# A narrow transpose placed before ScalarE's cast of its PSUM bank, and a multiplication placed three steps later

## The chip, the cores and the metric

The kernel runs on one core of a Trainium2 chip. The metric is the device time of one execution in microseconds (us); a change is given against the median of three runs. TensorE is called PE here (its weight loads PEld), VectorE DVE, ScalarE ACT, GpSimd POOL, and SyncE, which issues most DMAs, SP.

## The reference

Three layers follow one another, all in 32-bit floats:

- Attention over 2 batches x 8 heads, 768 tokens, head size 64. Each query and key gets a 6-bit bucket (the signs of its projections); a query sees only keys of its bucket: `scores = where(q_bucket == k_bucket, q k^T / 8, -1e9)`, then a softmax over the keys and a product with v.
- `x = relu(x @ w_in)**2 @ w_out` with 1536 tokens, 512 features and 2048 hidden units.
- The same shapes again with `h * sigmoid(h)` in place of the squared relu.

## The kernel before

The 16 heads are worked in 8 pairs. A pair has 4 units (head h, query half z of 384), a unit has 3 score tiles (128 queries x 768 keys) and 6 key blocks of 128. The attention is a software pipeline of steps d (`for d in range(-5, G // 2 + 3)`, L1258): 12 steps per pair, step 12(p+1) being the first step of the pair after p. In each step the program emits, engine by engine in this order:

- DVE: the row maximum of the score tile made in the step before (L996), the low part of the previous key block (`t_lo`, L1036), two small operations that make scale and bias of the exponential (L1000, L1001), then `t_lo` of the step's first block.
- PE: for two key blocks three 128x128 transposes each of the exponentials P (`transp`, L1025) into PSUM tiles `t` (three bank-sized buffers); four matmuls of v with the transposed blocks two behind (`av`, L1049, L1050); and four matmuls of the next score tile (`score_mm`, L989; its third and fourth use the rows of the bucket bits in `qq` and `kk`).
- ACT: the high part of each transposed block (`t_hi`, L1030, a cast out of the bank), and the exponential (L1009), which also gives the row sums.

A product is kept to float precision by splitting operands into a high and a low part.

Once per pair there is a long step, at 12(p-1)+5 for the pair p to come: PE also computes the projections of its queries and keys (`bits_mm`, 12 matmuls, L789), DVE compares them with zero (`bits_cmp`, L795, after a first `t_lo`, with the second `t_lo` between the two compares), and SP sends the bits to their rows of `qq` and `kk` (`place_bits`, L919, the `kk` part second). The first score that reads them is issued two steps later. In the long steps 17, 29, 41, 53, 65 and 77 there are also one or two DVE operations that prepare weights of the next layer (`w_exp` L958, `w_sign` L962, `w_low` L966).

The softmax is normalised on the product side. `norm_rows` (step 2 of the next pair) takes the reciprocals of a pair's 12 columns of sums on DVE. For pairs 0 to 5 `row_turn` (step 5 of the next pair, so in the six long steps just named, called turns below) transposes them on PE into columns 384 to 511 of the bank of the step's second block, whose first 384 columns `t_hi` reads, and ACT copies them out. `row_put` sends them to DRAM, and three steps later `row_get` reads them back spread over 64 partitions each into `rw` (two buffers). `x_mul` (POOL, step 10) multiplies the pair's summed output `ta` (two buffers) by `rw` into `yf`; `x_put` (POOL, step 10) splits a part of that into `xk`, once for pairs 0 to 3 and twice for 4 and 5.

Each engine runs its own instructions in the order in which they are emitted. Behind `x_mul` and `x_put` on POOL come `split_pair` for the keys (L774, step 11), whose result SP sends on (L779, L780), `load_head` (L764, step 1 of the pair after, a DMA issued by POOL) and `x_sum` of the next pair (L1103, step 3 of that pair), which frees `tb` (one buffer) for DMAs that SP issues (L1062).

The lists `todo` (end of a step) and `mid` (inside it) hold what else a step emits; within a step of `todo` the entries of the loop over `p` in L1141 come first. After the attention PE starts the two layers; their order is planned once and is the same in both kernels.

Of the kernel before, what the change touches and what calls it, by code (L numbers as in the profile page):

```python
# [24 lines left out]
NPAIR = B * H // 2  # L25
NU = NPAIR * 4
QW = 384
# [672 lines left out]
def lsh_attention_moe_moe(ctx, tc, kd, qk, qf, fq, v, pc, wi1, wo1, wi2, wo2, out):  # L700
    nc = tc.nc
# [23 lines left out]
    ident = ac.tile([128, 128], F32, name="ident")  # L725
# [30 lines left out]
    def scale_q(p):  # L756
        q = pair[p]["r"][0]
        nc.scalar.mul(out=q, in_=q, mul=SCALE)
# [23 lines left out]
    def bits_mm(p):  # L782
        t = pair[p]
        hp, lp = t["hp"], t["lp"]
        ops = [(w[:, 48 * i : 48 * i + 48], x) for i in range(2) for (w, x) in ((pjh, hp[i]), (pjl, hp[i]), (pjh, lp[:, i]))]
        s = ps_s.tile([128, 2, 512], F32, tag="s", name=f"bs{p}")[:, 0], ps_t.tile([128, 512], F32, tag="t", name=f"bt{p}")
        for z in range(2):
            for j, (w, x) in enumerate(ops):
                mm(s[z][0:48, 0:QW], w, x[:, z * QW : (z + 1) * QW], start=j == 0, stop=j == 5)  # L789
        return s  # L790
# [185 lines left out]
    P, stats, otile, sums = {}, {}, {}, {}  # L976

    def warm_up(n):
        for _ in range(n):
            mm(warm, zb[:, 0:128], zb[:, 0:512], start=True, stop=True)  # L980
# [13 lines left out]
    def row_max(u, j, s):  # L994
        m = mt[:, (u * 3 + j) % 4]
        nc.vector.tensor_reduce(out=m[:, 0:1], in_=s[:, :, 0:QW], op=ALU.max, axis=AX.XY, negate=True)  # L996
        return m

    def row_live(m):
        nc.vector.tensor_scalar(out=m[:, 1:2], in0=m[:, 0:1], scalar1=LIM, scalar2=1.0, op0=ALU.is_lt, op1=ALU.mult)  # L1000
        nc.vector.tensor_scalar(out=m[:, 2:3], in0=m[:, 0:1], scalar1=LIM, scalar2=m[:, 0:1], op0=ALU.is_lt, op1=ALU.mult)  # L1001

    def score_exp(u, j, s, m):
        p = u // 4
        if u % 4 == 0 and j == 0:
            sums[p] = a2.tile([128, 12], F32, tag="sums", name=f"sums{p}")
        e = P[u, j] = ac.tile([128, S], F32, tag="P", bufs=6, name=f"P{u}_{j}")
        c = (u % 4) * 3 + j
        nc.scalar.activation(  # L1009
            out=e.rearrange("p (a b) -> p a b", a=2),  # L1010
            in_=s[:, :, 0:QW],
            func=AF.Exp,
            scale=m[:, 1:2],
            bias=m[:, 2:3],
            accum_out=sums[p][:, c : c + 1],
        )

    PT = {}

    def transp(g, t=None):  # L1020
        u, kt = divmod(g, KT)
        if t is None:
            t = ps_t.tile([128, 512], F32, tag="t", name=f"t{g}")
        for j in range(3):
            nc.tensor.transpose(t[:, j * 128 : (j + 1) * 128], P[u, j][:, kt * 128 : (kt + 1) * 128], ident)  # L1025
        PT[g] = (t,)

    def t_hi(g):
        th = a1.tile([128, QW], F32R, tag="th", bufs=6, name=f"th{g}")
        nc.scalar.copy(out=th, in_=PT[g][0][:, 0:QW])  # L1030
        PT[g] += (th,)

    def t_lo(g):
        t, th = PT[g]
        tl = a1.tile([128, QW], F32R, tag="tl", bufs=6, name=f"tl{g}")
        nc.vector.tensor_tensor(out=tl, in0=t[:, 0:QW], in1=th.bitcast(F32), op=ALU.subtract)  # L1036
        PT[g] = th, tl
# [3 lines left out]
    def av(g):  # L1041
        u, kt = divmod(g, KT)
        p, h, z = u // 4, (u // 2) % 2, u % 2
        if kt == 0:
            otile[u] = ps_o.tile([128, 512], F32, tag="o", name=f"o{u}") if u < NU - 1 else ps_s.tile([128, 2, 512], F32, tag="s", name=f"o{u}")[:, 0]
        o = otile[u]
        vv = pair[p]["vv"][:, h * KT + kt].rearrange("p a d -> p (a d)")
        th, tl = PT.pop(g)
        mm(o[:, 0:QW], vv, th, start=kt == 0, stop=False)  # L1049
        mm(o[:, 0:QW], vv, tl, start=False, stop=kt == KT - 1)  # L1050
        if kt == KT - 1:
            if p not in xs:
                xs[p] = [a1.tile([128, S], F32, tag=n, bufs=b, name=f"{n}{p}") for n, b in (("ta", 2), ("tb", 1))]
            if u == NU - 1:
                ta, zs = xs[p][0], slice(z * QW, (z + 1) * QW)
                nc.scalar.copy(out=ta[64:128, zs], in_=o[0:64, 0:QW])
                nc.vector.tensor_tensor(out=ta[64:128, zs], in0=o[64:128, 0:QW], in1=ta[64:128, zs], op=ALU.add)
                return
            ob = a2.tile([128, QW], F32, tag="ob", name=f"ob{u}")
            nc.scalar.copy(out=ob, in_=o[:, 0:QW])  # L1060
            for i in range(2):
                nc.sync.dma_start(out=xs[p][i][64 * h : 64 * h + 64, z * QW : (z + 1) * QW], in_=ob[64 * i : 64 * i + 64])  # L1062
# [10 lines left out]
            w = rows[p] = a1.tile([128, 6, 2, 64], F32, tag="rw", bufs=2, name=f"rw{p}")  # L1073
            nc.gpsimd.tensor_copy(out=w, in_=ri.rearrange("p (h c) -> p c h", h=2).unsqueeze(3).broadcast_to([128, 6, 2, 64]))

    def row_turn(p, t):
        nc.tensor.transpose(t[0:12, QW:512], sums[p], ident)
        r = turned[p] = a1.tile([12, 128], F32, tag="rt", name=f"rt{p}")
        nc.scalar.copy(out=r, in_=t[0:12, QW:512])

# [54 lines left out]
    long, scale, turn = {}, {}, {}  # L1135
    last = defaultdict(list)

    def at(g, fn, *a):
        todo[g].append((fn, a))
# [21 lines left out]
    for p in range(NPAIR):  # L1161
        d0 = 12 * (p + 1)
        at(d0 + (-3 if p < NPAIR - 1 else -4), norm_sums, p)
        at(d0 + (2 if p < NPAIR - 1 else -3), norm_rows, p)
        at(d0 + (3 if p < NPAIR - 1 else 0), x_sum, p)
        if p == NPAIR - 2:
            extra[d0 + 9].append((rb_mm, x_norm, p))
            at(d0 + 10, x_mul, p)
            at(d0 + 10, x_put, p)
        elif p < NPAIR - 2:  # L1170
            k = d0 + 5
            turn[k] = p
            at(k, row_put, p)
            at(k + 3, row_get, p)
            at(k + 5, x_mul, p)
            at(k + 5, x_put, p)

    for k, d in enumerate(X_STEPS):
        at(d, x_form, k)
# [14 lines left out]
    with tc.manual_schedule():  # L1194
# [15 lines left out]
        c, k = slice(64, 64 + NBR), first["c"]  # L1210
# [47 lines left out]
        for d in range(-5, G // 2 + 3):  # L1258
            ready, new = new, None
            g = 2 * d  # L1260
            if ready:
                m = row_max(*ready)
            if 0 <= g - 1 < G and g - 1 not in early_lo:
                t_lo(g - 1)
            if ready:
                row_live(m)
            for fn, a in mid.pop(d, []):
                fn(*a)
            if 0 <= g < G and d in (92, 94):
                t = ps_s.tile([128, 2, 512], F32, tag="s", name=f"t{g}")  # L1270
                for i in range(2):
                    transp(g + i, t[:, i])
                t_hi(g)
                t_hi(g + 1)
                t_lo(g)
            elif 0 <= g < G:
                transp(g)
                t_hi(g)
                t_lo(g)
                transp(g + 1)  # L1280
                t_hi(g + 1)
                if d in turn:
                    row_turn(turn[d], PT[g + 1][0])
            more = extra.pop(d, [])
            if ready and more and d not in long:
                score_exp(*ready, m)
            if d in long:
                score_exp(*ready, m)
                if d in scale:
                    scale_q(scale.pop(d))  # L1290
            for n in (g - V_LAG, g + 1 - V_LAG):
                if 0 <= n < G:
                    av(n)
            if d in long:
                t = bits_mm(long[d])
            held = [(dve, pe(p), p) for pe, dve, p in more]
            if d in long:
                bits_cmp(t, long[d], 0)
                t_lo(g + 1)
                bits_cmp(t, long[d], 1)  # L1300
            for dve, t, p in held:
                dve(t, p)
            if ready and not more and d not in long:
                score_exp(*ready, m)
            u, j = divmod(d + 5, 3)
            if u < NU:
                new = u, j, score_mm(u, j)
            for fn, a in todo.pop(d, []) + last.pop(d, []):
                fn(*a)
            warm_up(WARM.get(d, 0))  # L1310
        p = NPAIR - 1
        for z in (1, 0):
            t = ps_t.tile([128, 512], F32, tag="t", name=f"rb{p}_{z}")
# [12 lines left out]
        t = dict(yf=yf, xk=xk, wpa=wpa, raw=raws, wt=wt, pair=both, src=((wi1, wo1), (wi2, wo2)), out=out)  # L1326
# [58 lines left out]
```

## Time and profile before

| what | value |
|---|---|
| median of 3 runs (lowest to highest) | 729.46 us (729.27 to 729.68) |
| the profiled execution | 728.33 us, span from first to last instruction 726.6 us |
| busy share of the span: PE, PEld, DVE, ACT, POOL | 98%, 84%, 84%, 74%, 36% |
| chain that ended last | PE 80%, DVE 15%, ACT 3%, issue 1% |
| granted TensorE clock | 1.000 |
| end of the attention | about 235.3 us |

The busy shares are means over both stages. The chain of waits goes back from the last instruction to what released each one. A row of a timeline gives the start, the duration, the engine, the line, the operation with its tiles, and in brackets how long the engine had been idle before it and what ended that; rows of instructions of one line that follow each other are merged (x6). Matmuls are pipelined: a row's duration is longer than the time to the next start.

### The profile page before, as it was taken

The numbers are of one execution on the slowest core, as the hardware profiler recorded it, in microseconds if no ns is written. First come the engines' busy times: TensorE is split into PE (matmuls) and PEld (weight loads), VectorE is DVE, ScalarE is ACT, GpSimd is POOL, SyncE is SP. The second block draws the span as 40 slices with busy tenths as digits, with TensorE's granted clock in tenths as the row PEclk, the third lists the DMA queues.
The fourth block names the chain that finished last, engine by engine and source line by source line (L and its number), as shares of the span: only waits on it lengthen the run. The fifth ranks groups of instructions, "written<-read, shape, count | busy, mean of one in ns | idle before, by whom it ended". The sixth has DMA issues, their size and how long they took to land.

```text
span 726.6 us, 10910 instructions
## 1 busy us (share of the span) xinstructions
PE 714.7 (98%) x3643; PEld 612.2 (84%) x3643; DVE 610.8 (84%) x1106; ACT 539.7 (74%) x1012; POOL 258.7 (36%) x242
## 2 busy tenths in 40 slices
PE   8999999999999999999999999999999999999998
PEld 4999898898899888888888888888788888888886
DVE  7999999999998979786797879989778778888840
ACT  6998898898798898486459568878766945854861
POOL 7634755656547512041231223234203110212300
PEclk9999999999999999999999999999999999999999
DMA  5887698697662536124534653368231332345432
GB/s 172 202 199 169 158 204 187 153 222 175 147 157 55 122 107 169 59 73 102 130 88 116 133 134 96 87 143 172 70 124 58 88 89 80 107 102 116 102 110 93
DMA packets 38640, 92.16 MB, mean 127 GB/s; under 512 B 5564, under 2 KB 10524, under 8 KB 38584
## 3 DMA queue, kind: packets, MB, share of 16 engines
q1 hardware_dynamic: 26120, 67.18, 31.7%
q0 software_dynamic: 12032, 23.79, 18.3%
q8 instruction: 29, 0.48, 0.3%
q10 hardware_dynamic: 432, 0.49, 0.2%
q14 instruction: 27, 0.22, 0.1%
HBM read 51.96 MB, written 3.18 MB: 76 GB/s over the span
## 4 chain that ended last, share of the span: by engine, by line
PE 80%; DVE 15%; ACT 3%; issue 1%; DMA 0%; POOL 0%; ACTq 0%; DVEq 0%; POOLq 0%
PE bank L558 36%; PE bank L443 24%; DVE mt L996 7%; PE bank L420 7%; DVE tl L1036 6%; PE s L989 3%; PE t L1025 3%; PE o L1049 2%; PE o L1050 2%; ACT P L1009 2%; PE bs L789 1%; PE bt L789 1%; DVE mt L1001 1%; ACT th L1030 1%; DVE mt L1000 1%
## 5 line engine op out<-in xcount | busy, mean ns | idle before, releaser
L558 PE MATMUL bank<-woh,cell 128*128 128x512 f32 (+1 forms) x392 | 120.0, 385 | 0.0
L558 PE MATMUL bank<-cell,woh 128*128 128x512 f32 x384 | 118.3, 389 | 0.0
L1036 DVE TENSOR_TENSOR tl<-t,th 128x384 fp32r<-128x384 f32 x192 | 104.7, 548 | 0.8 <-ACT th L1030 0.8
L1009 ACT ACTIVATE P<-s,mt 128x768 f32<-128x768 f32 x96 | 95.3, 993 | 11.2 <-DVE mt L1001 8.1
L996 DVE TENSOR_REDUCE mt<-s 128x1 f32<-128x768 f32 x96 | 91.5, 953 | 3.5 <-PE s L989 3.1
L1030 ACT CAST th<-t 128x384 fp32r<-128x384 f32 x192 | 81.9, 483 | 12.5 <-PE t L1025 12.1
L558 PEld LDWEIGHTS bank<-woh,cell 128*128 128x128 f32 x392 | 73.1, 188 | 14.7
L558 PEld LDWEIGHTS bank<-cell,woh 128*128 128x128 f32 x384 | 72.1, 188 | 15.2
L989 PE MATMUL s<-kk,qq 76*128 76x384 f32 (+1 forms) x384 | 83.8, 339 | 0.5 <-ACT P L1009 0.4
L1025 PE MATMUL t<-ident,P 128*128 128x128 f32 x576 | 78.9, 272 | 0.0
L278 DVE TENSOR_TENSOR cell<-bank,cell 128x512 f32<-128x512 f32 x91 | 62.1, 692 | 18.3 <-PE bank L443 13.9
L443 PE MATMUL bank<-xw,wpb 128*128 128x512 f32 x312 | 75.9, 389 | 0.0
L558 PE MATMUL bank<-wol,cell 128*128 128x512 f32 (+1 forms) x196 | 75.4, 385 | 0.0
L558 PE MATMUL bank<-cell,wol 128*128 128x512 f32 x192 | 74.7, 389 | 0.0
L1049 PE MATMUL o<-th,vv 128*128 128x384 f32 x192 | 72.5, 377 | 0.0
L1025 PEld LDWEIGHTS t<-ident,P 128*128 128x128 f32 x576 | 67.8, 140 | 4.5 <-DVE tl L1036 0.2
L989 PEld LDWEIGHTS s<-kk,qq 76*128 76x128 f32 (+1 forms) x384 | 68.3, 188 | 2.6 <-ACT P L1009 1.6
L443 PEld LDWEIGHTS bank<-xw,wpb 128*128 128x128 f32 x312 | 58.5, 188 | 12.4 <-DVE bank L278 0.3
L1050 PE MATMUL o<-tl,vv 128*128 128x384 f32 x192 | 64.3, 335 | 0.0
L588 ACT COPY yf<-bank 128x512 f32<-128x512 f32 x48 | 27.9, 586 | 35.4 <-PE bank L558 34.7
L450 ACT COPY cell<-bank 128x512 f32<-128x512 f32 x39 | 22.9, 587 | 40.7 <-PE bank L443 38.7
L268 ACT CAST cell<-cell 128x512 fp32r<-128x512 f32 x81 | 48.8, 617 | 1.9 <-DMA cell<-cell 0.8
(201 smaller groups left out, 1484.8 us busy)
## 6 DMA issues: line engine op xcount, KB each, us to landing
raw<-in_dram SPq DMA_DIRECT2D x64, 512.0 KB
cell<-cell POOLq DMA_DIRECT2D x23, 256.0 KB, 3.4
qq<-hq SPq DMA_DIRECT2D x28, 192.0 KB
kk<-in_dram POOLq DMA_DIRECT2D x14, 384.0 KB, 5.3
yf<-cell POOLq DMA_DIRECT2D x21, 256.0 KB, 3.3
vr<-in_dram SPq DMA_DIRECT2D x8, 384.0 KB
ta<-ob SPq DMA_DIRECT2D x31, 96.0 KB
tb<-ob SPq DMA_DIRECT2D x31, 96.0 KB
```

What stands on the lines that cost most here:

```text
L278: add("DVE", 0.70, lambda: vec.tensor_tensor(out=val(out), in0=bank[b], in1=val(other), op=ALU.add), [("bank", b), *reads], writes)
L420: mm(bank[b], wpa[n][:, p, 4 * h + j], x[:, q], start=j == 0 and z == 0, stop=j == 3 and z == 2)
L443: mm(bank[b], w[:, p], x[:, q], start=not started and z == 0, stop=z == 2, skip_group_check=started)
L558: mm(bank[b][:, 0:wd], x, y, start=start and i == 0 and z == 0, stop=i == (FB if half is None else 2 * half + 2) - 1 and z == 2, skip_grou ...
L989: mm(s[:, n, 0:QW], t["qq"][h][0:kk, ab, c0 : c0 + 128], t["kk"][h][0:kk, ab, n * QW : (n + 1) * QW], start=ab == 0, stop=ab == 1)
L996: nc.vector.tensor_reduce(out=m[:, 0:1], in_=s[:, :, 0:QW], op=ALU.max, axis=AX.XY, negate=True)
L1009: nc.scalar.activation(out=e.rearrange("p (a b) -> p a b", a=2), in_=s[:, :, 0:QW], func=AF.Exp, scale=m[:, 1:2], bias=m[:, 2:3], accum_ou ...
L1025: nc.tensor.transpose(t[:, j * 128 : (j + 1) * 128], P[u, j][:, kt * 128 : (kt + 1) * 128], ident)
L1030: nc.scalar.copy(out=th, in_=PT[g][0][:, 0:QW])
L1036: nc.vector.tensor_tensor(out=tl, in0=t[:, 0:QW], in1=th.bitcast(F32), op=ALU.subtract)
L1049: mm(o[:, 0:QW], vv, th, start=kt == 0, stop=False)
L1050: mm(o[:, 0:QW], vv, tl, start=False, stop=kt == KT - 1)
```

## The change

Two things change. The narrow transpose of the reciprocals is issued by PE right behind the transposes of the second block, ahead of the program's `t_hi` of that block; ACT's copy of its result stays behind `t_hi`. And for pairs 0 to 4 `x_mul` goes from step 10 to step 13 (counted from the start of the next pair, so step 1 of the one after), and `x_put` from step 10 to step 14. Pair 5 keeps both at step 10.

```diff
-    def row_turn(p, t):
-        nc.tensor.transpose(t[0:12, QW:512], sums[p], ident)
+    def row_copy(p, t):
         r = turned[p] = a1.tile([12, 128], F32, tag="rt", name=f"rt{p}")
         nc.scalar.copy(out=r, in_=t[0:12, QW:512])
...
-            at(k + 5, x_mul, p)
-            at(k + 5, x_put, p)
+            x = k + (8 if p < NPAIR - 3 else 5)
+            at(x, x_mul, p)
+            at(x + 1 if p < NPAIR - 3 else x, x_put, p)
...
                 transp(g + 1)
+                if d in turn:
+                    nc.tensor.transpose(PT[g + 1][0][0:12, QW:512], sums[turn[d]], ident)
                 t_hi(g + 1)
                 if d in turn:
-                    row_turn(turn[d], PT[g + 1][0])
+                    row_copy(turn[d], PT[g + 1][0])
```

## Rows read from the trace of the kernel before

**Rows 1.** Busy time by engine in the stretch behind the attention (PE, PEld, DVE, ACT, POOL).

```profile
235.30:726.60 491.30, 487.56 (x2161) 403.38 (x2159) 389.32 (x578) 336.43 (x568) 118.70 (x107) 1.00 0.41 107
```

**Rows 2.** Who waited for whom: total us, times, longest.

```profile
PE t L1077 <- ACT th L1030: 6.2, 6, 1.0
```

**Rows 3.** Timeline of PE, step 16, the turn in step 17, and step 19.

```profile
50.59 0.82 PE L1025 MATMUL t<-ident,P 128*128 128x128 f32 x6
...
51.95 0.86 PE L989 MATMUL s<-kk,qq 128*128 128x384 f32 x4
52.64 0.82 PE L1025 MATMUL t<-ident,P 128*128 128x128 f32 x6
54.50 0.27 PE L1077 MATMUL t<-ident,sums 128*12 128x128 f32 x1 [1.04 <-ACT th L1030]
...
55.31 0.33 PE L789 MATMUL bs<-hq,pjh 128*48 128x384 f32 x1
...
57.40 0.88 PE L989 MATMUL s<-kk,qq 128*128 128x384 f32 x4
...
61.54 0.69 PE L989 MATMUL s<-kk,qq 128*128 128x384 f32 x3
```

**Rows 4.** Timeline of DVE, the row maximum in step 19.

```profile
60.38 0.96 DVE L996 TENSOR_REDUCE mt<-s 128x1 f32<-128x768 f32 x1 [0.34 <-PE s L989]
```

**Rows 5.** Timeline of ACT in the turn of step 17.

```profile
53.50 0.86 ACT L1030 CAST th<-t 128x384 fp32r<-128x384 f32 x2
54.81 0.26 ACT L1079 COPY rt<-t 12x128 f32<-12x128 f32 x1 [0.45 <-PE t L1077]
```

**Rows 6.** Timeline of DVE in the turns of steps 17, 29 and 77.

```profile
55.43 0.55 DVE L1036 TENSOR_TENSOR tl<-t,th 128x384 fp32r<-128x384 f32 x1
56.56 0.67 DVE L795 TENSOR_SCALAR bt<-bs,tmt 48x384 fp32r<-48x384 f32 x1 [0.58 <-PE bs L789]
...
82.46 0.68 DVE L966 SCALAR_TENSOR_TENSOR wi<-raw,wi 128x512 uint32<-128x512 uint32 x1
...
83.40 0.55 DVE L1036 TENSOR_TENSOR tl<-t,th 128x384 fp32r<-128x384 f32 x1
84.66 0.67 DVE L795 TENSOR_SCALAR bt<-bs,tmt 48x384 fp32r<-48x384 f32 x1 [0.71 <-PE bs L789]
...
194.90 1.70 DVE L966 SCALAR_TENSOR_TENSOR both<-raw,both 128x512 uint32<-128x512 uint32 x1
...
196.86 0.55 DVE L1036 TENSOR_TENSOR tl<-t,th 128x384 fp32r<-128x384 f32 x1
197.32 0.66 DVE L795 TENSOR_SCALAR bt<-bs,tmt 48x384 fp32r<-48x384 f32 x1
```

**Rows 7.** Timeline of SP's DMA issues in the same three long steps.

```profile
59.15 1.06 SPq L919 DMA_DIRECT2D kk<-bt  x1
...
87.27 0.76 SPq L919 DMA_DIRECT2D kk<-bt  x1
...
199.91 0.77 SPq L919 DMA_DIRECT2D kk<-bt  x1
```

**Rows 8.** Line L989 after steps 29 and 77: PE sequencer's waits, ns, start us.

```profile
L989 PEldq EVENT_SEMAPHORE  x1: 752/752/752, 88.8 to 88.8; - x1
...
L989 PEldq EVENT_SEMAPHORE  x1: 857/857/857, 201.4 to 201.4; - x1
```

**Rows 9.** Timeline of PE, the first scores of a pair after steps 29 and 77.

```profile
89.64 0.68 PE L989 MATMUL s<-kk,qq 128*128 128x384 f32 x3
...
202.07 0.86 PE L989 MATMUL s<-kk,qq 128*128 128x384 f32 x4
```

**Rows 10.** Timeline of POOL before the turn of step 77.

```profile
185.96 1.84 POOL L1115 TENSOR_TENSOR yf<-rw,ta 128x768 f32<-128x768 f32 x1 [6.39 <-DMA rw<-rows]
...
191.72 1.85 POOL L774 TENSOR_TENSOR lp<-rk,hk 128x768 fp32r<-128x768 f32 x1
...
194.20 1.84 POOL L1103 TENSOR_TENSOR ta<-ta,tb 128x768 f32<-128x768 f32 x1
```

## The prediction

> **What bounds the kernel now.** I read the page first (busy shares and the chain that ended last, in the table above), then busy time by stretch, then who waited for whom, and then timelines of one turn and the steps around it, engine by engine. Behind the attention PE is busy 487.56 of 491.30 us [rows 1]: that stage is TensorE back to back, so whatever the attention saves should reach the end unchanged. In the list of waits the reader is to look for PE as the one that waits: the narrow transpose waited for ACT's cast six times, 6.2 us in all, the longest 1.0 [rows 2]. All six turns are therefore alike.
>
> Who sets the pace of a plain step? PE's starts repeat after 2.05 us (50.59 to 52.64) [rows 3]. Of that the score takes 0.69 (51.95 to 52.64), and four value matmuls 0.70, at the 0.174 that one 384-column matmul of the projections takes (twelve from 55.31 to 57.40) [rows 3]. That leaves 0.66 for the six transposes, 0.11 each. DVE needs nearly as long, but two steps after the turn it stands idle for 0.34 us until PE has a score ready [rows 4]. PE leads, DVE follows closely. An engine that follows by so little may take over when PE gets faster, so both are followed below.
>
> **The transpose.** In the turn of step 17 PE begins its six transposes at 52.64; they occupy it for 0.66, so it could go on at 53.30. The narrow transpose starts at 54.50 [rows 3]. PE loses 1.20 us; the 1.04 in the row is smaller because the profile lets the last transpose end later. Nothing else in the step waits: ACT's second cast, which held the bank, runs from about 53.93 to 54.36 [rows 5]. Moved ahead of that cast, the narrow transpose needs only the reciprocals, made three steps earlier. It follows at 53.30 and still costs its 0.11. Six turns give 6 x 1.20 = 7.2 us.
>
> The wait turns round: now the second cast waits for the narrow transpose. Behind it on ACT stand the copy (0.26), the exponential and the rest of the step. PE finishes the narrow transpose at about 53.30 + 0.27 = 53.57, and the second cast could not begin before 53.93 since the first one runs until then [rows 5]. It is covered with about 0.36 to spare; uncovered it would delay an engine that idles 0.45 right there [rows 5]. I cost it at nothing. ACT's copy then loses its 0.45 of waiting and the exponential starts earlier.
>
> **What is late next: the bits.** With PE 1.20 earlier, the projections, the compares on DVE, SP's two DMAs and the first score that reads them all want to move up by 1.20. DVE cannot quite. In step 17 its `t_lo` at 55.43 hands on after 0.46 (196.86 to 197.32, where nothing waits), so the first compare can start at 55.89 instead of 56.56: 0.67 earlier, not 1.20. In step 29, 83.40 + 0.46 = 83.86 against 84.66: 0.80 earlier [rows 6]. What follows (second compare, DMA issues, landing) moves with the compare.
>
> How much slack had the bits? PE's sequencer sat in a semaphore wait for them until 88.8 + 0.75 = 89.6 and until 201.4 + 0.86 = 202.23 [rows 8]; the issues of the `kk` bits ended at 88.03 and 200.68 [rows 7]. So they land 1.55 to 1.57 us after the issue ends. In the first turn that gives 59.15 + 1.06 + 1.56 = 61.77, 0.23 after the score's first matmul at 61.54, and PE's row shows no wait [rows 3, 7]; the third matmul is the first to read them. I take 0.2 after the first matmul as the deadline. Then the slack was about 0 in step 17, 89.84 - 89.6 = 0.24 in step 29, and 202.27 - 202.23 = 0.04 in step 77 [rows 8, 9].
>
> So PE gets a new wait two steps after each turn. Step 17: 1.20 - 0.67 - 0 = 0.53. Step 29, and step 53 with the same two weight operations: 1.20 - 0.80 - 0.24 = 0.16 each. Step 77 depends on the next part and gives 0.14. Steps 41 and 65, with one weight operation, I take at 0.1 each. Sum 1.2 us. Its bounds: nothing, if the DMA issue shortens or the landing is quicker (the issue ran from 0.76 to 1.06 [rows 7]), and 6 x 1.20 = 7.2 if the compares do not move at all. I take 1.2, which lies nearest to the rows of the turns themselves.
>
> **x_mul and x_put.** POOL is told to multiply at step 10, before the rows are back from DRAM, and stands idle: 6.39 us before the multiplication of pair 4 [rows 10]. Behind it wait the key split and the DMA of the next head, then `x_sum`. The only one of PE's waits that is large is the one for ACT's cast [rows 2]; none is for POOL. So the stall itself costs nothing and its removal gives nothing directly. In number: five `x_mul` of 1.84, and `x_put` pairs of a cast and a subtraction, move past one key split and one head load each, no SP instruction of their own; no work is added. The split and its two SP DMAs come earlier by several us, with no reader before the next pair.
>
> There is one indirect effect. In step 77 the weight operation L966 took 1.70 us; in step 29 it took 0.68. At 194.90, when it started, POOL was in `x_sum` (194.20 to 196.04), late because of the queue before it [rows 6, 10]. L966 ends 0.56 after POOL does, as if held until then. Here a rule of the Trainium skill bears (SBUF — State Buffer, section "Who interferes with whom"): a VectorE instruction with two SBUF inputs and a GpSimd one that reads SBUF lock each other out for a whole instruction. The trace agrees, 1.70 against 0.68; by the rule each such meeting after the change would again cost about 1.0.
>
> After the move the order for pair 4 is split, load (both early), `x_mul` at the landing of the rows, two `x_put`, `x_sum`. The multiplication and the `x_put`s take 191.72 - 185.96 = 5.76, so `x_sum` starts at 191.72 instead of 194.20 and ends at 193.56, all on one shifted clock; L966 starts at 194.90 [rows 6, 10]. They miss each other by 1.3 us. L966 then takes 1.02 less, the compare is free 1.02 earlier, and the new wait there is 1.20 - 1.02 - 0.04 = 0.14, used above. Without the move it would be 1.16: that is what the move is worth, about 1 us.
>
> **Sum.** 7.2 - 1.2 = 6.0 us less. Against the profiled execution: 728.33 - 6.0 = 722.3. That execution was 1.13 below the median of the runs, and the same difference put back gives 729.46 - 6.0 = 723.5.
>
> **Rivals.**
>
> *A. The bits cost nothing.* The issues in the first turn shorten to the 0.76 of the others and the landing follows. For it: two of three issues took 0.76 [rows 7]. Against it: DVE moves by 0.67 to 0.80 where PE moves by 1.20. Time 729.46 - 7.2 = 722.3.
>
> *B. DVE and POOL meet more often.* If `x_sum` or `x_put` now runs while a weight operation of a turn starts, the compare is late by up to 1.0 there, and PE waits for the bits. For it: it happened in step 77 [rows 6, 10]. Against it: the queue ends 1.3 us ahead. With two to four such meetings the gain is 6.0 - 2 to 4 x 1.0: 725.5 to 727.5. The Trainium skill's rule on the shared port, named above, is the rule behind this case.
>
> *C. The wait is not removed but moved.* If PE's narrow transpose, in its new place, still waits for a cast (the first block's, or the bank's earlier reader), or the second cast becomes late enough to hold `t_lo`, PE loses its 1.2 elsewhere. For it: the wait list names only the last releaser. Against it: the bank was already being written by PE. Time 729.5, no change.
>
> *D. Slower.* `x_sum` of the next pair now stands behind `x_mul` and `x_put` at steps 13 and 14. If the rows land late, `x_sum` holds `tb`, SP's copy into `tb` waits, and behind it in SP's queue stand the bits of the turn, which PE needs. It decides from the point where `x_sum` ends more than about 5 us later than worked out: 1.3 until the turn and some 4 from there to SP's bits in step 17 (54.50 to 59.15 [rows 3, 7]). Each us beyond is paid in full by PE. With 3 us in three turns the loss is 9 against the gain of 6.0: 732.5. Against it: `x_sum` comes 2.5 us earlier, not later [rows 10].
>
> **Chances.** The forecast 0.62, A 0.15, B 0.14, C 0.05, D 0.04. About 0.2% (1.5 us) is what a measurement of this kernel can tell from no change. Faster: the forecast, A and nearly all of B, 0.91. Same: C and the rest of B, 0.06. Slower: most of D, 0.03. The likeliest case by itself spans 722.6 to 724.5 (a new wait of 0.4 to 2.2). The range reaches to A below, with half a microsecond for the reading of the 1.20, and into B above: 721.8 to 726.0.
>
> **What would show it.** The wait of L1077 for ACT's cast is gone from the list, and PE issues it about 0.1 before the first value matmul. PE shows a new wait in L989 two steps after each turn, largest after step 17 (about 0.5), about 1.2 in all. The step of a turn, from its first transpose to that of the next step, shortens by 1.2. L966 in step 77 takes 0.68. `x_mul` waits some 10 to 15 us in all for its rows, mostly for pair 5. The stretch behind the attention stays at 491.3. I am wrong if L1077 still waits, if a score waits over 0.6 after several turns, or if a weight operation in a turn takes over 1 us.

## The result and the profile after

The changed kernel took 722.98 us (median of four executions) where the kernel before took 729.37 (728.88 to 729.68) on the same chip: a ratio of 0.991 [0.9891, 0.993]. The forecast was 723.5, with a range of 721.8 to 726.0. The changed kernel was run again beside the first experiments, and there it took 723.35 (722.92 to 723.68) against 729.29: 0.9918 [0.9904, 0.9931]. All rows "after" come from that second measurement, since in the first one the profiled execution took 1025.15 us at a granted clock of 0.655 from end to end, where the other three took 722.42 to 723.05. The profiled execution of the second took 723.39 us, with a span of 721.6.

First the chain that ended last. Before, PE held 80% of it, DVE 15% and ACT 3%. After, from the page of the changed kernel:

```profile
PE 91%; DVE 7%; DMA 1%; ACT 0%; issue 0%; SPq 0%; DVEq 0%; ACTq 0%
```

ACT's cast is gone from it, DVE's share has halved, and a DMA is there that was not before. The timeline of PE shows what became of the turn (the first projections of step 5, the turn of step 17, the score two steps later, the same in step 67, and the first projections of step 77):

```profile
27.89 0.33 PE L789 MATMUL bs<-hq,pjh 128*48 128x384 f32 x1
...
53.33 0.82 PE L1025 MATMUL t<-ident,P 128*128 128x128 f32 x6
53.99 0.27 PE L1282 MATMUL t<-ident,sums 128*12 128x128 f32 x1
...
54.80 0.33 PE L789 MATMUL bs<-hq,pjh 128*48 128x384 f32 x1
...
61.08 0.51 PE L989 MATMUL s<-kk,qq 128*128 128x384 f32 x2
61.84 0.62 PE L989 MATMUL s<-kk,qq 76*128 76x384 f32 x2 [0.25 <-DMA kk<-bt]
62.30 0.82 PE L1025 MATMUL t<-ident,P 128*128 128x128 f32 x6
...
169.56 0.51 PE L989 MATMUL s<-kk,qq 128*128 128x384 f32 x2
170.37 0.59 PE L989 MATMUL s<-kk,qq 76*128 76x384 f32 x2 [0.30 <-DMA qq<-bt]
...
190.76 0.33 PE L789 MATMUL bs<-hq,pjh 128*48 128x384 f32 x1
```

The six transposes begin at 53.33 and take 0.66, and the narrow one, now L1282, follows at 53.99 with no bracket of idle time. In [rows 3] it stood 1.20 later than that. By the same reading the six turns had lost 7.18 us, and now lose nothing; the list of waits names no wait of L1282. Two steps later the score, which should hold PE for 0.69, holds it from 61.08 to 62.30, 1.22: its third matmul, the first to read the bits, came 0.52 late. The bracket says 0.25 because it counts the idle time from the modelled end of the matmul before. So measured, the new waits after the six turns are 0.52, 0.15, 0, 0.18, 0.54 and 0.14, together 1.53.

From the first projection of step 5 to that of step 77 it is now 162.87 us (27.89 to 190.76), before 168.63 (27.21 to 195.84): 5.76 less. The removed 7.18 less the new waits up to there (1.53 less the last 0.14) makes 5.79. The account closes. Over all six turns it is 7.18 - 1.53 = 5.65.

The stretch behind the attention, by windows (columns as in [rows 1]), is as long as before within 0.2 us:

```profile
230.10:721.60 491.50, 487.82 (x2163) 403.59 (x2161) 389.32 (x578) 336.93 (x569) 119.08 (x108) 1.00 0.42 107
```

On DVE the first compare of step 17 stands where `t_lo` leaves it, with no idle time for PE's projection as in [rows 6]; all six instructions hand on without a gap, so there DVE, and no longer PE, decides when the compares come:

```profile
55.05 0.42 DVE L958 TENSOR_SCALAR wi<-wi 128x512 uint32<-128x512 uint32 x1
55.51 0.69 DVE L962 SCALAR_TENSOR_TENSOR wi<-raw,wi 128x512 uint32<-128x512 uint32 x1
56.12 0.55 DVE L1036 TENSOR_TENSOR tl<-t,th 128x384 fp32r<-128x384 f32 x1
56.58 0.66 DVE L795 TENSOR_SCALAR bt<-bs,tmt 48x384 fp32r<-48x384 f32 x1
57.17 0.54 DVE L1036 TENSOR_TENSOR tl<-t,th 128x384 fp32r<-128x384 f32 x1
57.63 0.66 DVE L795 TENSOR_SCALAR bt<-bt,tmt 48x384 fp32r<-48x384 f32 x1
...
163.58 0.95 DVE L962 SCALAR_TENSOR_TENSOR both<-raw,both 128x512 uint32<-128x512 uint32 x1
...
191.01 0.68 DVE L966 SCALAR_TENSOR_TENSOR both<-raw,both 128x512 uint32<-128x512 uint32 x1
```

L966 in step 77 takes 0.68 (1.70 in [rows 6]). POOL's `x_sum` before it and before step 65, and POOL's two long waits in the list (total, times, longest):

```profile
162.14 1.84 POOL L1102 TENSOR_TENSOR ta<-ta,tb 128x768 f32<-128x768 f32 x1 [1.34 <-DMA tb<-ob]
...
188.10 1.85 POOL L1102 TENSOR_TENSOR ta<-ta,tb 128x768 f32<-128x768 f32 x1
```

```profile
POOL yf L1114 <- DMA rw<-rows: 11.8, 3, 8.4
POOL ta L1102 <- DMA tb<-ob: 10.7, 6, 5.6
```

`x_mul` waited 41.2 us for its rows in six waits before; now 11.8 in three. What I had not foreseen is the second row: `x_sum`, no longer stuck behind the queue, now waits for the DMA that brings its own operand into `tb` (5.3 us in two waits before). In step 65 that DMA puts it at 162.14 to 163.98, across the start of the weight operation at 163.58.

### The profile page after: what moved, and what is told of

Read it like the earlier page. It is cut to its first block, busy times and chain, and to the rows that moved or that the text cites. A ratio compares the mean times of both kernels' runs of the same rounds, so it can differ in the third digit from the quotient of the medians.

```text
span 1023.4 us, 10903 instructions
## 1 busy us (share of the span) xinstructions
PE 1018.4 (100%) x3642; PEld 704.0 (69%) x3643; DVE 612.0 (60%) x1106; ACT 558.0 (55%) x1012; POOL 257.4 (25%) x242
## 4 chain that ended last, share of the span: by engine, by line
PE 100%; DVE 0%; issue 0%; DVEq 0%
PE bank L558 37%; PE bank L443 25%; PE s L989 9%; PE t L1025 9%; PE bank L420 7%; PE o L1049 5%; PE o L1050 5%; PE bt L789 1%; PE bs L789 1%; PE warm L980 1%; PE bf L884 0%; PE bs L900 0%; PE t L1282 0%; PE rb L1317 0%; PE rb L1096 0%; DVE yf L594 0%
## 5 line engine op out<-in xcount | busy, mean ns | idle before, releaser
L558 PE MATMUL bank<-woh,cell 128*128 128x512 f32 (+1 forms) x392 | 161.8, 501 | 0.0
L558 PE MATMUL bank<-cell,woh 128*128 128x512 f32 x384 | 160.0, 508 | 0.0
L989 PE MATMUL s<-kk,qq 76*128 76x384 f32 (+1 forms) x384 | 111.9, 426 | 0.0
L1025 PE MATMUL t<-ident,P 128*128 128x128 f32 x576 | 111.0, 346 | 0.1
L443 PE MATMUL bank<-xw,wpb 128*128 128x512 f32 x312 | 107.2, 506 | 0.0
L1025 PEld LDWEIGHTS t<-ident,P 128*128 128x128 f32 x576 | 86.7, 162 | 18.0
L558 PE MATMUL bank<-wol,cell 128*128 128x512 f32 (+1 forms) x196 | 97.5, 497 | 0.0
L558 PE MATMUL bank<-cell,wol 128*128 128x512 f32 x192 | 96.9, 504 | 0.0
L1049 PE MATMUL o<-th,vv 128*128 128x384 f32 x192 | 92.8, 483 | 0.0
L989 PEld LDWEIGHTS s<-kk,qq 76*128 76x128 f32 (+1 forms) x384 | 78.7, 207 | 16.5 <-issue 0.7
L558 PEld LDWEIGHTS bank<-wol,cell 128*128 128x128 f32 x196 | 41.0, 209 | 22.3 <-issue 7.2
```

The costliest lines, as they stand in the source:

```text
L443: mm(bank[b], w[:, p], x[:, q], start=not started and z == 0, stop=z == 2, skip_group_check=started)
L558: mm(bank[b][:, 0:wd], x, y, start=start and i == 0 and z == 0, stop=i == (FB if half is None else 2 * half + 2) - 1 and z == 2, skip_grou ...
L989: mm(s[:, n, 0:QW], t["qq"][h][0:kk, ab, c0 : c0 + 128], t["kk"][h][0:kk, ab, n * QW : (n + 1) * QW], start=ab == 0, stop=ab == 1)
```

## The experiments

Each was measured beside the kernel before. e1 to e4 shared one chip and its runs of before (729.29), e5 to e8 another (729.14), e9 and e10 a third (728.85). Each has 4 or 5 executions, e3 and e10 have 11. Where an edit adds or takes away lines, the line numbers of its rows are shifted (by 7 in e4 and e7 to e9).

### e1: the changed kernel again

No edit. 

> The changed kernel itself, for a profile at the full clock and a closer time. My theory (PE loses its six waits of 1.20 us, and gets a new wait for the bucket bits two steps after each turn): 723.0 (722.5 to 723.5) against 729.4; L1077 no longer waits for ACT; PE waits in L989 about 0.5 us after step 17 and 1.2 in all; L966 in step 77 takes 0.68. Rival A (bits cost nothing): the same time is then made of a wait removed of about 6.4 and no wait in L989. Rival B (DVE held by POOL more often): weight operations of 1 us or more in several turns.

Measured 723.35; its rows are those above.

### e2: the transpose alone

```diff
-            x = k + (8 if p < NPAIR - 3 else 5)
-            at(x, x_mul, p)
-            at(x + 1 if p < NPAIR - 3 else x, x_put, p)
+            at(k + 5, x_mul, p)
+            at(k + 5, x_put, p)
```

> Only the narrow transpose is moved; x_mul and x_put stay at step 10. My theory: PE gains as in the full change, but L966 in step 77 is still held by x_sum on POOL (1.70 us) and L962 in step 65 in part (1.08 us), the compares there stay late, and PE waits for the bits: some 1.0 and 0.4 us more, 724.4 (723.8 to 724.9). Rival (the move of x_mul is worth nothing): 723.0, as the full change.

Measured 725.05 (723.74 to 726.25), 0.9945 [0.9932, 0.9957]: 1.7 us above the whole change, and just above what was expected. The move is thus worth somewhat more than the 1 us I gave it, by runs that spread over 2.5 us, but not where I had put it. L966 in step 77 took only 0.93 here. The collision had gone to step 65; the timelines of POOL, DVE and PE there:

```profile
162.44 0.66 POOL L764 DMA_DIRECT2D kk<-in_dram  x1
163.13 1.87 POOL L1102 TENSOR_TENSOR ta<-ta,tb 128x768 f32<-128x768 f32 x1
```

```profile
163.11 2.45 DVE L962 SCALAR_TENSOR_TENSOR both<-raw,both 128x512 uint32<-128x512 uint32 x1
```

```profile
164.94 0.88 PE L989 MATMUL s<-kk,qq 128*128 128x384 f32 x4
166.08 0.55 PE L1025 MATMUL t<-ident,P 128*128 128x128 f32 x3 [0.26 <-DVE tl L1036]
167.21 0.52 PE L1025 MATMUL t<-ident,P 128*128 128x128 f32 x3 [0.59 <-DVE tl L1036]
167.49 0.42 PE L1049 MATMUL o<-th,vv 128*128 128x384 f32 x1
```

The weight operation takes 2.45 us, `t_lo` behind it is late, and PE, which in the changed kernel goes from this score to the value matmuls in 1.29 us, needs 2.55 (164.94 to 167.49): 1.26 lost. This profiled execution (725.01) was 1.6 longer than the changed kernel's, although its first projections came 0.65 earlier (27.24 against 27.89). From there to the first projection of step 77 it took 1.53 longer (164.40 against 162.87), and the 1.26 is most of that. What is longer behind step 77 (0.7) is open.

### e3: the multiplication alone

The kernel before, with only this:

```diff
-            at(k + 5, x_mul, p)
-            at(k + 5, x_put, p)
+            x = k + (8 if p < NPAIR - 3 else 5)
+            at(x, x_mul, p)
+            at(x + 1 if p < NPAIR - 3 else x, x_put, p)
```

> Only x_mul and x_put are moved; the narrow transpose stays behind the cast. My theory: POOL no longer idles 41 us, but no wait of PE ends there, the narrow transpose still waits 1.0 us six times: 729.4, no change within 0.5. Rival (the queue behind x_mul is worth something by itself): 728.4 or less.

Measured 729.02 (728.39 to 729.72), 0.9995 [0.9987, 1.0004]: no difference. The waits of this kernel:

```profile
PE t L1077 <- ACT th L1030: 6.2, 6, 1.0
...
POOL yf L1115 <- DMA rw<-rows: 12.0, 3, 8.7
```

POOL's stall went from 41.2 to 12.0 us and the time did not follow, while PE's six waits stayed. L966 in step 77 fell from 1.70 to 0.68 too, and that gained nothing either, since PE had no wait for the bits there that could go. The move pays only together with the transpose.

### e4: the bits in three DMAs

PE's first score of a pair reads all `kk` bits but only the first half of the `qq` bits. This kernel is the changed one with those sent first; it asks whether the new wait is the way of the bits through SP.

```diff
-        last[d0 + 5].append((place_bits, (p, 0)))
+        last[d0 + 5].append((place_part, (p, 0, half(0))))
+        last[d0 + 5].append((place_part, (p, 1, slice(0, S))))
+        last[d0 + 5].append((place_part, (p, 0, half(1))))
```

(`place_part` is `place_bits` for one operand and a slice of its columns.)

> The changed kernel with the bits of a pair's first head sent as three DMAs: the half of the query bits that the first score reads, then the key bits, then the other half. The key bits' DMA is issued about 0.85 us earlier after the compares. My theory (PE waits for the key bits two steps after the turns): that wait goes, 721.8 (721.3 to 722.4) if it was 1.2 us. Rival A (the bits cost nothing): 723.0, no change; a third DMA issue on SP delays nothing.

Measured 722.16 (721.12 to 723.4), 0.9903 [0.9889, 0.9916], inside what was expected. On SP the `kk` bits are now issued at 57.64 to 58.41, in step 17, where they had been at 59.16 to 60.26; 0.68 of that is the later start of the changed kernel's profile, the other 0.84 is the edit. PE lost time to the bits only after step 41 (0.76) and step 65 (0.15). In step 41 a new meeting had come up, by DVE's, POOL's and PE's timelines:

```profile
108.22 1.32 DVE L969 SCALAR_TENSOR_TENSOR wi<-raw,wi 128x512 uint32<-128x512 uint32 x1
```

```profile
107.14 1.85 POOL L1109 TENSOR_TENSOR ta<-ta,tb 128x768 f32<-128x768 f32 x1 [2.03 <-DMA tb<-ob]
```

```profile
115.41 0.62 PE L996 MATMUL s<-kk,qq 76*128 76x384 f32 x2 [0.48 <-DMA kk<-bt]
```

So the new wait is the bits' wait, as predicted: with the bits issued earlier it is gone after steps 17, 29, 53 and 77, where it had been 0.98 in all. What is left, 0.91 against 1.53, comes from `x_sum`, whose time a landing DMA sets. The times alone do not show it: the medians lie 1.2 apart, but the runs of this kernel spread over 2.3 and the intervals of the two ratios overlap.

### e5: the move for one pair only

Is it only `x_mul` of pair 3, the one ahead of step 65, that the move has to take out of the way?

```diff
-            x = k + (8 if p < NPAIR - 3 else 5)
+            x = k + (8 if p == 3 else 5)
             at(x, x_mul, p)
-            at(x + 1 if p < NPAIR - 3 else x, x_put, p)
+            at(x + 1 if p == 3 else x, x_put, p)
```

> The narrow transpose moved, and x_mul and x_put moved for pair 3 alone, whose queue on POOL runs into the turn of step 65. My theory (the move is worth only what it keeps x_sum off the weight operation of a turn, and that was step 65 in the run with the transpose alone): L962 in step 65 takes under 1.2 us instead of 2.45, 723.5 (723.1 to 724.1), most of the 1.7 us between that run and the full change. Rival (all five moves count, by a shorter POOL queue): 724.5 to 725.0, near the run with the transpose alone.

Measured 725.18 (724.0 to 726.42), 0.9944 [0.9932, 0.9957]: a miss, and nearer to the rival. L962 in step 65 did fall to 0.68, as expected. But the collision moved on to step 77, where pair 4's `x_mul`, left at step 10, pushes `x_sum`. POOL, DVE and PE there:

```profile
190.24 0.68 POOL L764 DMA_DIRECT2D kk<-in_dram  x1
190.94 1.86 POOL L1102 TENSOR_TENSOR ta<-ta,tb 128x768 f32<-128x768 f32 x1
```

```profile
190.56 2.80 DVE L966 SCALAR_TENSOR_TENSOR both<-raw,both 128x512 uint32<-128x512 uint32 x1
```

```profile
194.22 0.55 PE L1025 MATMUL t<-ident,P 128*128 128x128 f32 x3 [0.94 <-DVE tl L1036]
195.36 0.52 PE L1025 MATMUL t<-ident,P 128*128 128x128 f32 x3 [0.59 <-DVE tl L1036]
```

PE reaches the value matmuls 1.95 late here (3.24 from the score's start at 192.40, in place of 1.29), and the clock then fell (last section), of which the other four executions show no sign (mean granted clock 0.999 to 1.000, 724.0 to 725.31 us). So moving pair 3 protected the turn of step 65, and the collision came up in another place. That every pair's move protects its own turn is not shown: in e2, with pair 4 as here, L966 in step 77 took only 0.93.

### e6: the weight operations one step later

If DVE's weight operations ahead of the compares are what keeps the bits late, taking them out of the turn should return the wait. The changed kernel with

```diff
-W_STEPS = ((0, 5, 17, 17, 29), (8, 17, 29, 41, 53), (30, 41, 53, 65, 77), (54, 65, 77, 92, 93))
+W_STEPS = ((0, 5, 18, 18, 30), (8, 17, 30, 42, 54), (30, 41, 54, 66, 78), (54, 65, 78, 92, 93))
```

> The full change with the weight operations of the turns (L958, L962, L966) emitted one step later. My theory (PE waits for the bits because DVE's compares cannot move up behind these operations): the wait in L989 two steps after the turns goes (1.5 to below 0.3 us), 721.9 if DVE pays nothing in the step after; DVE has 1.1 us more there against one t_lo less, so up to 0.3 per turn may come back: 721.9 to 723.3. Rival (the bits are late for another reason, the DMA alone): the waits in L989 stay at 1.5 us, 723.4 or more.

Measured 724.63 (724.02 to 725.05), 0.9937 [0.9924, 0.9949]: a miss, 1.3 slower than the changed kernel. The bits no longer hold PE anywhere. Instead PE waits for `t_lo`, in the list and in the timeline two steps after the turn:

```profile
PEld t L1025 <- DVE tl L1036: 3.3, 7, 0.7
...
PE t L1025 <- DVE tl L1036: 1.6, 4, 0.5
```

```profile
59.92 0.55 PE L1025 MATMUL t<-ident,P 128*128 128x128 f32 x3 [0.49 <-DVE tl L1036]
```

(The same edit moves POOL's casts of two finished weights, `wp_put`, a step later too.) The time alone would fit the rival, but its waits in L989 are not there. The buffers into which PE transposes are freed by `t_lo`, which now stands behind the weight operations (L962 at 58.70). PE lost 0.65, 0.52, 0.2, 0.52, 0.19 and 0.52 after the six turns, 2.6 in all. The theory that DVE had room one step later falls.

### e7: e4 and e6 together

The changed kernel with e4's three DMAs and e6's line:

```diff
-        last[d0 + 5].append((place_bits, (p, 0)))
+        last[d0 + 5].append((place_part, (p, 0, half(0))))
...
-W_STEPS = ((0, 5, 17, 17, 29), (8, 17, 29, 41, 53), (30, 41, 53, 65, 77), (54, 65, 77, 92, 93))
+W_STEPS = ((0, 5, 18, 18, 30), (8, 17, 30, 42, 54), (30, 41, 54, 66, 78), (54, 65, 78, 92, 93))
```

> The bits in three DMAs and the weight operations one step later, both. My theory: no wait for the bits is left in either way, so this adds nothing to the better of the two: 721.8 to 722.8. Rival (the two remove different waits): 721.0 or less.

Measured 724.14 (723.72 to 724.72), 0.9932 [0.9919, 0.9944]: a miss for the same reason. The waits for `t_lo` are those of e6 within 0.02, and earlier bits have nothing left to give.

### e8: e4 with the weight operations behind both compares

```diff
-            for fn, a in mid.pop(d, []):
-                fn(*a)
+            if d not in long:
+                for fn, a in mid.pop(d, []):
+                    fn(*a)
...
                 bits_cmp(t, long[d], 1)
+                for fn, a in mid.pop(d, []):
+                    fn(*a)
```

> The bits in three DMAs, and the weight operations in the same step behind both compares. My theory: the compares are never held, and no x_sum on POOL meets a weight operation before them, so no turn loses anything: 721.3 (720.9 to 722.0), unless the weight operations meet the casts of the next queries on POOL, are stretched to 1 us or more, and make the next row maximum late: then 722 to 723. Rival (the third DMA costs what it saves): 723.0 or more.

Measured 723.94 (723.67 to 724.3), 0.9929 [0.9916, 0.9943]: the worse of the two outcomes I had allowed, and beyond it. The time lies in the rival's range, but the wait is not one of SP's third DMA; it is e6's:

```profile
PEld t L1032 <- DVE tl L1043: 3.1, 7, 0.9
```

PE lost 0.86, 0.45, 0.12, 0.45, 0.12 and 0.40. The turns with one weight operation (41 and 65) lose 0.12, those with two 0.40 to 0.86: DVE has room for one of them behind the compares, not for two.

### e9: the same in two turns only

e8 with `if d not in (41, 65):`, so the turns with two weight operations keep them ahead of the compares.

> The bits in three DMAs; in the turns of steps 41 and 65 alone the one weight operation is emitted behind both compares, in the others it stays. My theory (what is left in the kernel with three DMAs is the turn of step 41 or 65 when x_sum on POOL holds the weight operation, 1.32 us and a PE wait of 0.75 in its profile; behind the compares it cost 0.12): PE waits under 0.4 us in all, 721.6 (721.2 to 722.3), and the runs lie closer together than 721.1 to 723.4. Rival (nothing is gained, DVE pays the same later): 722.2 to 722.8.

Measured 721.64 (721.29 to 721.98) against 728.85, 0.9899 [0.9886, 0.9912], the time as expected. PE loses 0.16 after step 17, 0.22 after 41 and 0.17 after 65, 0.55 in all where under 0.4 was expected, and nothing after the others; the list keeps little of the wait for `t_lo`:

```profile
PEld t L1032 <- DVE tl L1043: 0.6, 3, 0.2
```

Its median lies 7.2 below that of the kernel before, the changed kernel's 6.4 and 5.9 below: the largest gain of the kernels run, 0.8 to 1.3 us more than the changed kernel's. The lead is small: single runs of e9 gained 6.9 to 7.6, those of the changed kernel 5.6 to 6.9, and the intervals of the two ratios overlap. From e4 (7.1) its median is not told apart; its runs lie within 0.7 us, where e4's spread over 2.3.

### e10: the multiplication behind the next pair's sum

Three steps more: `x_mul` then runs into the turn, and this is also a place at which rival D could show.

```diff
-            x = k + (8 if p < NPAIR - 3 else 5)
+            x = k + (11 if p < NPAIR - 3 else 5)
```

> The full change with x_mul at step 16 and x_put at step 17 (11 and 12 steps behind the turn's base) in place of 13 and 14, so that they follow x_sum on POOL just before the next turn. My theory (POOL work with SBUF operands holds a weight operation with two SBUF inputs): the weight operations of steps 29 to 77 start while x_mul or x_put runs, take 1.2 us or more in at least three turns, PE waits for DVE or the bits 0.5 to 2 us in each, 725 to 730. Rival (only x_sum by its DMAs matters, or POOL and DVE do not hold each other): 723.4, as the full change.

Measured 727.98 (725.2 to 729.79), 0.9986 [0.9975, 0.9997]: nearly the whole gain is gone, as expected. The weight operations were held in every turn from step 29 on: 0.93 and 2.07 in step 29, 1.67, 1.32 and 0.96 in the next three, 0.72 and 1.51 in step 77. DVE and POOL in the turn of step 29:

```profile
81.62 0.93 DVE L966 SCALAR_TENSOR_TENSOR wi<-raw,wi 128x512 uint32<-128x512 uint32 x1
82.47 2.07 DVE L958 TENSOR_SCALAR wi<-wi 128x512 uint32<-128x512 uint32 x1
```

```profile
81.97 2.29 POOL L1114 TENSOR_TENSOR yf<-rw,ta 128x768 f32<-128x768 f32 x1
```

L958 takes 0.41 to 0.46 in the other kernels' turns. Behind the held operations PE waits for `t_lo`. From the list of waits, and PE before step 68:

```profile
PE t L1025 <- DVE tl L1036: 2.5, 5, 0.7
...
PEld s L989 <- DMA qq<-bt: 2.3, 1, 2.3
```

```profile
174.53 0.59 PE L989 MATMUL s<-kk,qq 76*128 76x384 f32 x2 [2.04 <-DMA qq<-bt]
```

Around step 65 SP issued nothing from 161.94 to 168.70: the next copy in its queue (L1062, into `ta`) had to wait for `x_mul`, which ended at 168.67. The bits stand behind that copy. This is D's mechanism, with another tile than the `tb` that I had named. It cost 2.3 us, once (step 67); by PE's timeline about 3.5 us more were lost in the turns to the late `t_lo` and in the step behind each. So the larger part of the loss is the one that the expectation named, a DVE held by POOL. Several of the other executions had a mean granted clock of 0.997 to 0.998, which this one (0.999) does not show.

## Why the prediction was right

**The transpose, 7.2 removed: right.** 7.18 by the same rows. The 1.20 that I read off one turn held for all six (1.18 to 1.20). Rival C, a wait only moved, is excluded: L1282 begins the moment the six transposes end.

**The second cast, at nothing: right.** ACT's copy and exponential follow without a wait that PE could see, and PE has no wait for ACT's cast left.

**The new wait, 1.2: right in kind, 0.3 too small.** Step 17 was forecast at 0.53 and measured 0.52; 29: 0.16 and 0.15; 41: 0.1 and 0; 53: 0.16 and 0.18; 77: 0.14 and 0.14. The mis-sized term is step 65: 0.1 against 0.54. I had taken steps 41 and 65 as alike because each has one weight operation, without reading their rows; that 0.1 had no working, and that it came out in step 41 is luck. DVE in step 65 of the kernel before:

```profile
166.78 1.08 DVE L962 SCALAR_TENSOR_TENSOR both<-raw,both 128x512 uint32<-128x512 uint32 x1
167.78 0.55 DVE L1036 TENSOR_TENSOR tl<-t,th 128x384 fp32r<-128x384 f32 x1
168.95 0.67 DVE L795 TENSOR_SCALAR bt<-bs,tmt 48x384 fp32r<-48x384 f32 x1 [0.63 <-PE bs L789]
```

L962 took 1.08 (166.78 to 167.86) and not 0.68, beside an `x_sum` that ran from 165.47 to 167.30. So `t_lo` began at 167.78 and the compare, then at 168.95, could come no more than 168.95 - 168.24 = 0.71 earlier against PE's 1.20. My own method on that row gives about 0.5. (One sum of the slack is printed from a rounded row: 201.4 + 0.86 is 202.26. The wait began at 201.375 and ended at 202.23, so the 0.04 holds.) The chain from compare to bits held: in step 17 the compare came 0.66 earlier (0.67 forecast), after allowing for the start-up below, and the landing 1.56 after the issue's end gives 59.16 + 1.10 + 1.56 = 61.82 for a matmul that began at 61.84. e4 shows that it is this path: with the path shortened, the wait went where the compares were not held. Rival A, bits at no cost, is thereby wrong for this change, and e4 and e9 are what it takes to come near its 722.3.

**The move of x_mul: near in size, wrong in place.** Nothing by itself (e3), as forecast; 1.7 us with the transpose (e2), forecast about 1. I had read the collision off step 77 of the kernel before and moved it by a common shift. In step 77 of the changed kernel the margin is as forecast (`x_sum` ends at 189.95, L966 starts at 191.01: 1.06, forecast 1.3). But with the transpose alone the heavy meeting is in step 65, because POOL's times hang on DMA landings and don't shift along with PE's, and it costs PE by a late `t_lo`, not by the bits. That the size came near is in part luck. One meeting of rival B's kind is left in the changed kernel, step 65's 0.95, but it is no new one (1.08 before). B's further meetings stayed away.

**The sum: 6.0, measured 6.4 and 5.9** as differences of medians, 5.65 by the account of the profiled execution. The range held the time. By the account the forecast is 0.35 too high, from the new wait; why the medians differ by more than the account is open. Rival D did not occur here, and e10 shows that its mechanism exists three steps further on.

**What stays open.** In the profiled execution the span fell by 5.0 only, since its first projections came 0.68 late (27.89 against 27.21). The delay arises at the start, far ahead of the change (last section). e3's profile has it too, with 27.80. I have no cause for it. Why some executions of e2 and e5 take 2.4 us more than others is open: one execution of each is profiled. For e5 that was its slowest, and the stretch of low clock shown below is about 1.6 of it.

## What to carry to other kernels

When a wait of the leading engine goes, work out for each follower how far it can move by itself, place by place and from that place's own rows: here five of six came out within 0.1 us, and of the three taken by analogy with another turn (41, 53 and 65) one was off by 0.44. An instruction moved off the second-leading engine's path has to land where that engine has room, or the wait only changes its name (e6 to e8). A stall on an engine with time to spare is worth nothing by itself, and still its removal can be worth something by where the instructions behind it then fall.

## What was unexpected of the hardware

**What holds a DVE operation.** A weight operation (L962 or L966, two SBUF inputs) that started inside a POOL `TENSOR_TENSOR` ended about 0.55 after it: 0.55 in e4, 0.56 in the kernel before. In e2 and e5 it started before POOL's by the profile, by 0.02 and 0.38, and was held all the same, for 2.45 and 2.80; it ended 0.56 after POOL's again (in step 77 of e5 192.80 to 193.36). In e5 POOL was issuing a DMA (L764) when it started, and in e2 that issue had ended less than 0.01 before. Behind the attention of the changed kernel there is a third case: an L962 that started at 240.15, inside a DMA issue of POOL (239.72 to 240.58), took 2.31, while the one just ahead of it, which started 0.18 before that issue, took 0.68. Whether the issue itself holds DVE until POOL's next operation is not shown: in no run did a weight operation start inside an issue with no `TENSOR_TENSOR` behind it.

POOL's operation matters too. Beside a `TENSOR_SCALAR` L962 was not held in e6: it took 0.69 at 58.70 while POOL ran one from 57.23 to 59.16. In step 17 of e8, though, it took 0.98 beside one, and that is open. Beside a cast it took 0.72 to 0.74 in e8 to e10, but these casts ended 0.18 after it had begun, and it ended 0.54 to 0.55 after each, as with a `TENSOR_TENSOR`; so the casts are not shown to leave it free. And L958, with one SBUF input, was held as well in e10, for 2.07. The Trainium skill (SBUF — State Buffer, section "Who interferes with whom") states an exclusive lock on the port pair shared by VectorE and GpSimd. The traces agree that the two shut each other out, but not beside the `TENSOR_SCALAR` of e6, and an earlier start by the profile did not protect DVE's.

**The clock after a stall.** In e5, after PE had stood idle for 0.94 and 0.59 us, PE's granted clock fell, by windows (columns as in [rows 1]; the clock is the third from the end):

```profile
194.00:196.00 2.00, 1.19 (x8) 0.98 (x9) 2.00 (x5) 0.51 (x2) 0.00 (x0) 1.00 0.88 241
196.00:198.00 2.00, 2.00 (x9) 1.91 (x8) 1.40 (x4) 1.44 (x3) 0.00 (x0) 0.52 0.15 30
198.00:199.50 1.50, 1.50 (x8) 1.50 (x7) 1.30 (x2) 0.42 (x2) 0.93 (x2) 0.50 0.14 25
199.50:202.00 2.50, 2.50 (x18) 2.47 (x18) 1.80 (x6) 2.27 (x7) 2.36 (x2) 1.00 0.68 165
```

PE had been busy for 1.19 of 2.00 us in the window before. Then the clock was for 3.5 us at about half, the 1.2 GHz level. From the first value matmul behind the stall to the score of the next step PE took 4.42 us (195.64 to 200.06), in the changed kernel 2.85 (194.14 to 196.99): the stall cost about 1.6 more than itself. It did not follow every stall: the clock stayed at 1.00 after the 2.04 of e10 and after e2's 0.26 and 0.59.

**The start.** The first matmul of L884 took 0.86 us in the changed kernel's profile and 0.37 before, the next three rows of it 0.60, 0.92 and 0.52 against 0.40, 0.57 and 0.40; the first of these began at 6.04 instead of 5.30, with the granted clock at 1.00 in both profiles, and about that much was still missing at the first projections. The instructions of that stretch are the same in both. In e9's profile the first one took 0.87 and the rest as long as before, and 0.22 was missing at the first projections (27.43).
